# An earlier weight load and a later slot for weight sums in a gated attention and gMLP kernel

## The chip, the cores and the metric

The kernel runs on one core of a Trainium2 (trn2) chip. The metric is the device time of one execution in microseconds (us), lower is better. Engines: PE is TensorE (matmuls), DVE is VectorE, ACT is ScalarE, SP is SyncE, which here issues the DMAs. "Granted clock" is the share of full speed that TensorE was allowed in an execution.

## The reference

The result mixes a sliding-window dilated attention (32 heads, window 8, dilation 2) with a gMLP block, row by row, by a sigmoid gate. S is 2048, D is 1024, half the gMLP width is 1792.

```python
qkv = x @ wqkv                                   # attention over 8 keys, 2 apart
attn = softmax(q . k[s - 2*w] * Dh**-0.5)        # w = 0..7, masked at the start
a = (attn . v[s - 2*w]) @ wo
z = gelu(x @ w_in)                               # [2048, 3584]
z1, z2 = z[..., :1792], layernorm(z[..., 1792:])
g = w_sp @ z2 + b_sp[:, None]                    # the "spatial" product
b = (z1 * g) @ w_out
return gate * a + (1 - gate) * b
```

## The kernel before

All large products are done as Strassen-type blocks: seven products of four matmuls in place of eight. That costs additions on DVE: sums of the weights before the products (line 577), and additions of a PSUM bank and a shared term between them (line 506, in `plus`). PE may go on accumulating into that bank only when `plus` is done.

```python
def chain(...):                                   # one block of seven products
    def plus(out, a):
        dve(N / 960.0 + 0.14, clock["PE"] + 0.2)
        last_add[0] = nc.vector.tensor_tensor(out[:, n], a[:, n], vs, ALU.add)   # line 506
    # ...
    product(Y, pairs(S2, T2), False, N)
    with tc.high_priority():
        plus(Z, Y)
    # ... later a product accumulates into Z

def sums4_steps(s_out, a11, a12, a21, a22):       # sums of weights, line 577
    # four nc.vector.tensor_tensor
```

While it is built, the kernel runs a small list scheduler with a clock of its own for each engine. It decides which piece of attention work (maxima of the scores, weights, products with v: lines 671 to 717) or which sum of weights comes next on DVE. The order it finds is fixed in the program. An instruction that waits holds up all behind it: in the trace of before DVE stood 2.79 us at a sum whose weights had not landed, and did nothing else.

```python
def dve(dur, ready):
    if live[0]:
        advance(ready)            # fill DVE with other work that starts before `ready`
    return take("DVE", dur, ready)

def advance(t):
    while True:
        # ...
        events += [(max(o[0], clock["DVE"]) + FR * o[1], 2 + n, o) for n, o in enumerate(options())]
        events = [v for v in events if v[0] <= t]
        # ... the smallest goes next; `fill` holds the sums of weights
```

The sums of the z2 weights enter that list when their load has landed by the planned clock:

```python
def landed(t):
    land[0] += 1
    if land[0] == KT:
        fill.extend((t + LATE, 1.05, f) for f in wz_sums(p))
```

The z1 stage runs seven passes (fp = 0 to 6). During it SP also issues transposes of w_sp (`load_raw`), stores z1 (`z_d` in the trace) and loads further w1 blocks; ahead of the transposes it stores the result of attention (`o_d`):

```python
RAW_AT = {2: {2: 0, 4: 1, 6: 2}, 3: {4: 3, 6: 4}, 4: {2: 5, 4: 6, 6: 7}}
for fp in range(NFH):
    # ...
    run(z1_quad(fp, 0), z1_quad(fp, 1), hooks={..., **{n: lambda a=a: load_raw(0, a) for n, a in RAW_AT.get(fp, {}).items()}}, step=...)
    # ...
    if fp in (0, 2):
        load_w1(fp + 3)                           # two halves of 512 KB
```

After the eight transposes DVE forms the sums of the spatial weights: lines 1126 and 1127, later 1129 and 1130.

Of the kernel before, what the change touches and what calls it, by code (L numbers as in the profile page):

```python
# [27 lines left out]
ZC = 448  # L28
# [30 lines left out]
def kernel(  # L59
# [177 lines left out]
    def pe(dur, ready=0.0):  # L237
        return take("PE", dur, ready)
# [3 lines left out]
    def table(name):  # L242
        if tables[0] != name:
            take("ACT", 1.28)
        tables[0] = name
        return 0.0

    def act(dur, ready):
        if live[0]:
            advance(ready)  # L250
        return take("ACT", dur, ready)
# [6 lines left out]
    def dma(ready, dur, f, landed=None, timed=False):  # L258
        if not live[0]:
            return f()  # L260
        item = [ready, dur, f, landed, timed]
        due.append(item)
        return item
# [297 lines left out]
    def run(*quads, hooks={}, step=None):  # L561
        quads = list(quads)
        n = 0
        while quads:
            n += 1
            if n in hooks:
                hooks[n]()
            for q in list(quads):
                if next(q, 0) == 0:
                    quads.remove(q)  # L570
                elif step is not None:
                    step()

    def sums4_steps(s_out, a11, a12, a21, a22):
        args = ((s_out[0], a21, a22, ALU.add), (s_out[1], s_out[0], a11, ALU.subtract), (s_out[2], a11, a21, ALU.subtract),
                (s_out[3], a12, s_out[1], ALU.subtract))
        return [lambda a=a: nc.vector.tensor_tensor(*a) for a in args]  # L577
# [9 lines left out]
    def mark(bs, N=512, lo=0):  # L587
        for b in bs:
            pe((N - lo) / 2400.0)
            nc.tensor.matmul(b[:, lo:N], xT[:, 4, 0:P], xT[:, 4, 0:N - lo], start=(lo == 0), stop=True, skip_group_check=True)  # L590
# [48 lines left out]
        sync.dma_start(v_t, bass.AP(tensor=v_d.tensor, offset=v_d.offset + (g * (S + 16) + 2) * C, ap=[[NJ * C, P], [1, NJJ * C]]))  # L639


    FR, LATE = 0.4, 0.5
    t_bands, t_v = [FAR] * NG, [FAR] * NG
    sub_end, exp_end = [FAR] * NG, [FAR] * NG
    v_data = [0.0]
# [97 lines left out]
    weighed, fill = [0], []  # L743
# [42 lines left out]
    def drain():  # L786
        t = clock["PE"]
        while any(s[1] != () for s in streams) or due:
            t += 0.5
            advance(t)  # L790
# [10 lines left out]
    def load_wz(p):  # L801
        def part(k):
            for m in range(2):
                sync.dma_start(wz[p][m][:, k:k + 1], win_v[:, k:k + 1, FH + ZC * (2 * m + p):FH + ZC * (2 * m + p + 1)])
        return [lambda k=k: part(k) for k in range(KT)]


    def wz_sums(p):
        w = wz[p]
        return sums4_steps(wzs[p], w[0][:, 0:4], w[0][:, 4:8], w[1][:, 0:4], w[1][:, 4:8])  # L810
# [27 lines left out]
    def w1_half(fp, f):  # L838
        return w1_first[:, f] if fp == 0 else w1_pairs[(fp - 1) // 2 % 2][f][:, :, (fp - 1) % 2 * P:((fp - 1) % 2 + 1) * P]

    def load_w1(fp):
        for f in range(2):
            to = w1_first[:, f] if fp == 0 else w1_pairs[(fp - 1) // 2 % 2][f]
            sync.dma_start(to, win_v[:, :, HF * f + fp * P:HF * f + (fp + (2 if fp else 1)) * P])

# [17 lines left out]
    def square(n, x, junk):  # L863
        c = slice(x * HF, (x + 1) * HF)
        src = z2[:, z2_row(n), c]
        if junk is None:
            junk, src = z2[:, 7:16:8, ZC:2 * ZC], src.rearrange("p (a c) -> p a c", a=2)
        else:
            junk = junk[:, c]
        return nc.scalar.activation(junk, src, ACT.Square, accum_out=(s2, s2h)[x][:, n:n + 1])  # L870
# [109 lines left out]
    def step():  # L980
        advance(clock["PE"])
# [6 lines left out]
    def load_later(p, at, gap):  # L988
        land = [0.0]

        def landed(t):
            land[0] += 1
            if land[0] == KT:
                fill.extend((t + LATE, 1.05, f) for f in wz_sums(p))
        for n, f in enumerate(load_wz(p)):
            dma(at + gap * n, 0.65, f, landed, True)

# [46 lines left out]
    for n in range(0, len(quads), 2):  # L1044
        p, i = quads[n]
        if p == 1 or quads[n + 1][0] == 1:
            t = clock["PE"]
# [21 lines left out]
    def moments(n):  # L1069
        sl = slice(n, n + 4)  # L1070
        s1v = s1[:, 4 * n:4 * (n + 4)].rearrange("p (i c) -> p i c", c=4)
        nc.vector.tensor_tensor(s2[:, sl], s2h[:, sl], s2[:, sl], ALU.add)
        nc.vector.tensor_reduce(mean[:, sl], s1v, AX.X, ALU.add)
        nc.vector.tensor_scalar(mean[:, sl], mean[:, sl], 1.0 / FH, None, ALU.mult)
        nc.vector.tensor_tensor(var[:, sl], mean[:, sl], mean[:, sl], ALU.mult)
        nc.vector.scalar_tensor_tensor(var[:, sl], s2[:, sl], 1.0 / FH, var[:, sl], ALU.mult, ALU.subtract)
        nc.vector.tensor_scalar(var[:, sl], var[:, sl], 0.0, EPS, ALU.max, ALU.add)
        nc.gpsimd.tensor_tensor(rstd[:, sl], var[:, sl], cm05[:, sl], ALU.pow)
        fill.extend((clock["DVE"] + 2.5, 0.7, lambda m=m: normalize(m)) for m in range(n, n + 4))
# [29 lines left out]
    def load_raw(c, a):  # L1109
        row = 4 * c + (a % 4) + 8 * (a // 4)  # L1110
        inst = sync.dma_start_transpose(raw_slots[c][:, :, a, :], wsp_v[row])
        if c:
            tc.add_manual_dep(inst.ins, last_store[0].ins.name, NOSYNC, reason="behind the stores")
# [27 lines left out]
    z1s_slots = [[free(o + 2048 * r, 2048).rearrange("p (f a t) -> p f a t", f=2, a=2) for r in range(2)] for o in (T1_OFF, R_OFF + 16384)]  # L1141
    zv_slots = [free(R_OFF + 20480 + 1024 * r, 1024, F32) for r in range(2)]

    w1_left = [0]

    def w1_sums(fp):
        def one(f):
            f()
            w1_left[0] -= 1
        steps = [(0.0, 0.34, lambda f=f: one(f)) for f in w1_steps(fp)]  # L1150
        w1_left[0] += len(steps)
        fill[:0] = steps
# [5 lines left out]
    def z1_quad(fp, c):  # L1158
        a, b, s = w1_half(fp, 0), w1_half(fp, 1), ws_slots[fp % 2]
        z1s, vs = z1s_slots[fp == 3][c], zv_slots[c]  # L1160
        lo, hi = slice(512 * c, 512 * c + 512), slice(1024 + 512 * c, 1536 + 512 * c)

        def share(*a):
            last_share[0] = nc.vector.tensor_copy(*a)

        def gelu(f, a, bank):
            act(0.6 + table("gelu"), max(clock["PE"], clock["DVE"] if f + a == 2 else 0.0) + 0.2)
            last_gelu[0] = nc.scalar.activation(z1s[:, f, a, :], bank[:], ACT.Gelu_apprx_tanh)  # L1168

        def store():  # L1170
            dst = z1_d[c].rearrange("p (f t) -> p f t", f=NF)[:, fp:fp + NFH + 1:NFH, :]
            last_store[0] = sync.dma_start(dst, z1s.rearrange("p f a t -> p f (a t)"))

        return chain([a[:, k] for k in K4], [a[:, 4 + k] for k in K4], [b[:, 4 + k] for k in K4],
                     *[[s[:, q, k, :] for k in K4] for q in range(4)],
                     [xT[:, k, lo] for k in K4], [xT[:, 4 + k, lo] for k in K4], [xT[:, 4 + k, hi] for k in K4],
                     *[[x[:, k, lo] for k in K4] for x in xts], vs, gelu, nc.scalar.copy if fp < 2 else share, 512, lean=True, done=store)
# [4 lines left out]
    def z1_step(fp, at):  # L1182
        step()
        at[0] += 1
        if at[0] % 2 == 0 and squares:
            act(0.5, clock["PE"])
            square(*squares.pop(0), z1_junk)
        n = ready[0]
        if all(s[1] == () for s in streams) and n + 4 <= (squares[0][0] if squares else 16):
            fill.append((clock["ACT"] + 0.5, 1.0, lambda n=n: moments(n)))  # L1190
            ready[0] += 4
        if fp == NFH - 1 and at[0] == 2:
            fill.extend((0.0, 1.15, f) for f in wsp_sums(0, 1))

    mark([b[1] for b in bank_roles], 512, ZC)
    dma(clock["PE"] + 1.0, 2.9, lambda: load_w1(1), w1_landed(1))
    RAW_IN = 3.0
    DRAIN, SUMS = 1, NFH - 2
    RAW_AT = {2: {2: 0, 4: 1, 6: 2}, 3: {4: 3, 6: 4}, 4: {2: 5, 4: 6, 6: 7}}
    for fp in range(NFH):  # L1200
        while w1_left[0]:
            advance(max(clock["PE"], clock["DVE"]) + 0.5)
        if 0 < fp < NFH - 1:
            w1_sums(fp + 1)
        if fp == SUMS:
            fill.extend((clock["PE"] + RAW_IN, 1.15, f) for f in wsp_sums(0, 0))
        late = () if fp else [b[2] for b in bank_roles]
        at = [0]
        run(z1_quad(fp, 0), z1_quad(fp, 1), hooks={3: lambda: mark(late, 512, ZC), **{n: lambda a=a: load_raw(0, a) for n, a in RAW_AT.get(fp, {}).items()}},
            step=lambda: z1_step(fp, at))  # L1210
        if fp == DRAIN:
            drain()
        if fp in (0, 2):
            load_w1(fp + 3)
        if fp == NFH - 3:
            load_rows()
    while fill:
# [426 lines left out]
```

## Time and profile before

| | before |
|---|---|
| time of four runs | 656.74, 656.4, 658.04, 656.42 us |
| profiled span | 654.3 us |
| two stops of PE for line 506, near 193 and 325 us | 1.30 and 1.50 us |
| DVE waiting for the z2 weights and for the fifth w1 block | 2.79 and 3.78 us |

The lines behind this table stand in the prediction. This is DVE's timeline of the kernel before around the first stop (columns: start in us, time of the group in us, engine, line, operation, output and input, count; in brackets idle time before the group and what ended it):

```profile
191.81 0.29 DVE L692 TENSOR_TENSOR att_A<-att_L,att_r 128x256 f16<-128x256 f16 x1
192.02 1.22 DVE L712 TENSOR_TENSOR arena<-arena 128x2048 f16<-128x2048 f16 x1
193.16 1.16 DVE L506 TENSOR_TENSOR psum_all<-psum_all,arena 128x448 f32<-128x448 f32 x2
194.22 1.22 DVE L712 TENSOR_TENSOR arena<-arena 128x2048 f16<-128x2048 f16 x1
```

The addition that PE waits for starts at 193.16. One 1.14 us step of attention work (line 712, from 192.02 to 193.16) stands directly ahead of it, and a second one directly behind.

### The profile page before, as it was taken

What the parts mean: (1) busy time and instruction counts of PE and PEld (TensorE: products, weight loads), DVE (VectorE), ACT (ScalarE), POOL (GpSimd) and SP (SyncE); (2) the same over time, 40 slices, a digit from 0 to 9 for tenths busy, and PEclk for the clock granted to TensorE, in tenths of its full rate; (3) what the DMA queues carried; (4) which work ended last, traced back from release to release, by engine and by line L of the source; (5) the groups of instructions that cost most, each with busy time, mean ns of one, the idle gap of its engine ahead of it and who ended that gap; (6) DMA issues with size and microseconds to landing.
All of it is one profiled execution on the core that took longest, in us unless ns stands there. A gap on an engine that the chain in (4) does not pass through costs nothing.

```text
span 654.3 us, 11411 instructions
## 1 busy us (share of the span) xinstructions
PE 644.7 (99%) x4425; PEld 338.6 (52%) x4425; DVE 517.6 (79%) x820; ACT 298.3 (46%) x652; POOL 6.2 (1%) x15
## 2 busy tenths in 40 slices
PE   8999999999989999999999999999999999999998
PEld 4544467544445555444444444444444444868684
DVE  2533989999899999999799676887659999596862
ACT  4545677766677777799544212111121112202020
POOL 1000000000000000001000000000000000000000
PEclk9999999999999999999999999999999999999999
DMA  9988645697778003247995587559587465454501
GB/s 218 189 207 225 123 101 151 154 233 162 183 187 221 7 6 120 65 129 199 278 220 172 123 171 175 143 147 282 128 186 173 98 145 97 113 146 111 132 29 53
DMA packets 230198, 98.19 MB, mean 150 GB/s; under 512 B 177520, under 2 KB 217088, under 8 KB 230144
## 3 DMA queue, kind: packets, MB, share of 16 engines
q1 hardware_dynamic: 229856, 97.27, 61.7%
q8 instruction: 34, 0.56, 0.4%
q10 hardware_dynamic: 288, 0.20, 0.1%
q14 instruction: 20, 0.16, 0.1%
HBM read 45.10 MB, written 36.61 MB: 125 GB/s over the span
## 4 chain that ended last, share of the span: by engine, by line
PE 86%; DVE 5%; ACT 4%; DMA 2%; issue 1%; SPq 0%; DVEq 0%; ACTq 0%
PE psum_all L435 67%; PE psum_all L1468 8%; PE psum_all L294 7%; PE psum_all L304 3%; DMA arena<-in_B_w_in_dram 2%; ACT arena L870 1%; DVE arena L708 1%; PE psum_all L356 1%; ACT arena L1168 1%; DVE arena L577 1%; DVE psum_all L506 1%; DMA arena<-in_A_x_dram 1%; DVE arena L712 1%; ACT arena L815 0%; ACT arena L364 0%
## 5 line engine op out<-in xcount | busy, mean ns | idle before, releaser
L435 PE MATMUL psum_all<-arena 128*128 128x512 f16 (+6 forms) x2462 | 493.0, 362 | 3.9 <-DVE psum_all L506 2.8
L435 PEld LDWEIGHTS <-arena 128*128 128x128 f16 (+1 forms) x2462 | 239.7, 98 | 249.6 <-issue 5.7
L708 DVE TENSOR_TENSOR arena<-arena,att_A 128x2048 f16<-128x2048 bf16 x64 | 75.3, 1219 | 0.3
L294 PE MATMUL psum_all<-arena 128*128 128x512 bf16 x256 | 57.5, 379 | 0.0
L506 DVE TENSOR_TENSOR psum_all<-psum_all,arena 128x512 f32<-128x512 f32 (+1 forms) x74 | 48.0, 667 | 7.1 <-PE psum_all L435 4.9
L1468 PE MATMUL psum_all<-arena 128*128 128x256 f16 (+1 forms) x468 | 51.6, 273 | 0.0
L1468 PEld LDWEIGHTS <-arena 128*128 128x128 f16 x468 | 45.8, 98 | 5.5
L453 ACT COPY psum_all<-psum_all 128x512 f32<-128x512 f32 (+1 forms) x24 | 12.5, 519 | 67.2 <-PE psum_all L435 66.4
L815 ACT ACTIVATE arena<-psum_all 128x448 bf16<-128x448 f32 x64 | 34.3, 546 | 18.4 <-PE psum_all L435 9.0
L1168 ACT ACTIVATE arena<-psum_all 128x512 bf16<-128x512 f32 x56 | 31.0, 616 | 23.0 <-PE psum_all L435 8.0
L294 PEld LDWEIGHTS <-arena 128*128 128x128 bf16 x256 | 24.4, 98 | 28.4 <-issue 0.2
L712 DVE TENSOR_TENSOR arena<-arena 128x2048 f16<-128x2048 f16 x32 | 38.0, 1217 | 0.0
L364 ACT CAST arena<-psum_all 128x1988 f16<-128x1988 f32 (+3 forms) x25 | 34.0, 1359 | 2.7 <-PE psum_all L356 2.2
L577 DVE TENSOR_TENSOR arena<-arena 128x512 f16<-128x512 bf16 (+3 forms) x52 | 25.5, 521 | 7.1 <-DMA arena<-in_B_w_in_dram 6.6
L870 ACT ACTIVATE arena<-arena 128x896 bf16<-128x896 bf16 x32 | 30.9, 982 | 0.0
L297 ACT CAST arena<-psum_all 128x512 bf16<-128x512 f32 x32 | 18.8, 586 | 26.6 <-PE psum_all L294 26.5
L477 ACT COPY psum_all<-psum_all 128x512 f32<-128x512 f32 (+1 forms) x24 | 12.4, 518 | 37.5 <-PE psum_all L435 36.8
L581 DVE TENSOR_TENSOR arena<-arena 128x1024 f16<-128x1024 f16 (+2 forms) x17 | 12.1, 719 | 18.6 <-PE psum_all L435 15.7
L464 ACT COPY psum_all<-psum_all 128x512 f32<-128x512 f32 (+1 forms) x24 | 12.4, 517 | 25.8 <-PE psum_all L435 24.8
L459 ACT COPY arena<-psum_all 128x512 f32<-128x512 f32 (+1 forms) x24 | 12.7, 533 | 25.0 <-PE psum_all L435 22.9
L518 ACT COPY psum_all<-psum_all 128x512 f32<-128x512 f32 (+1 forms) x37 | 20.6, 573 | 5.0 <-PE psum_all L435 4.3
L304 PE MATMUL psum_all<-arena 128*128 128x385 bf16 x128 | 22.6, 327 | 0.0
(112 smaller groups left out, 521.5 us busy)
## 6 DMA issues: line engine op xcount, KB each, us to landing
arena<-v_d SPq DMA_DIRECT2D x8, 960.0 KB, 7.5
z_d<-arena SPq DMA_DIRECT2D x14, 512.0 KB, 4.0
arena<-z_d SPq DMA_DIRECT2D x14, 512.0 KB, 4.3
zg_d<-arena SPq DMA_DIRECT2D x56, 128.0 KB, 2.2
arena<-zg_d SPq DMA_DIRECT2D x32, 224.0 KB, 3.3
band_d<-arena SPq DMA_DIRECT2D x28, 248.5 KB, 4.1
arena<-in_A_wqkv_dram SPq DMA_DIRECT2D x16, 256.0 KB, 4.7
o_d<-arena SPq DMA_DIRECT2D x4, 1024.0 KB, 5.9
```

Of the source, the lines that this page charges most:

```text
L294: nc.tensor.matmul(ps[:], w[:, t, kt, :], xT[:, kt, 512 * c:512 * (c + 1)], start=(kt == 0), stop=(kt == KT - 1))
L304: nc.tensor.matmul(ps[:, 0:VP + 1], xT[:, kt, i * P:(i + 1) * P], wvp[:, kt, :], start=(kt == 0), stop=(kt == KT - 1))
L364: nc.scalar.copy(dst, src)
L435: nc.tensor.matmul(bank[:, 0:N], lhsT, rhs, start=(start and m == 0), stop=(m == n - 1), skip_group_check=True)
L506: last_add[0] = nc.vector.tensor_tensor(out[:, n], a[:, n], vs, ALU.add)
L577: return [lambda a=a: nc.vector.tensor_tensor(*a) for a in args]
L708: lambda ws=ws, in0=in0, in1=in1: tt(p5[:, ws], in0[:, ws], in1[:, ws], ALU.mult)), False
L712: lambda a=p3[:, ws], b=p3[:, ws.start + 4:ws.stop + 4]: tt(a, a, b, ALU.add)), not n
L815: nc.scalar.activation(z2[:, i + 8 * a, ZC * c:ZC * (c + 1)], bank[:, 0:ZC], ACT.Gelu_apprx_tanh, accum_out=s1[:, 4 * n + c:4 * n + c + 1])
L870: return nc.scalar.activation(junk, src, ACT.Square, accum_out=(s2, s2h)[x][:, n:n + 1])
L1168: last_gelu[0] = nc.scalar.activation(z1s[:, f, a, :], bank[:], ACT.Gelu_apprx_tanh)
L1468: nc.tensor.matmul(bank[:, h], l, r, start=(start and m == 0), stop=(m == len(ab) - 1), skip_group_check=True)
```

## The change

It has two parts. **Part 1** loads the fifth w1 block as its slot frees: one half inside the third pass, the other right after it, with the third transpose moved to the next pass and the two stores of this pass kept until after the loads. **Part 2** moves the ready time of the z2 sums 3.5 us later in the scheduler's clock. Neither adds or removes work.

```diff
-    FR, LATE = 0.4, 0.5
+    FR, LATE, WZ_LATE = 0.4, 0.5, 4.0
 ...
-                fill.extend((t + LATE, 1.05, f) for f in wz_sums(p))
+                fill.extend((t + WZ_LATE, 1.05, f) for f in wz_sums(p))
 ...
-        def store():
+        def store(now=False):
+            if fp == 2 and not now:
+                kept_stores.append(store)
+                return
 ...
-    RAW_AT = {2: {2: 0, 4: 1, 6: 2}, 3: {4: 3, 6: 4}, 4: {2: 5, 4: 6, 6: 7}}
+    RAW_AT = {2: {2: 0, 4: 1}, 3: {2: 2, 4: 3, 6: 4}, 4: {2: 5, 4: 6, 6: 7}}
 ...
+        if fp == 2:
+            hooks[6] = lambda: load_w1(5, (0,))
 ...
-        if fp in (0, 2):
-            load_w1(fp + 3)
+        if fp == 0:
+            load_w1(3)
+        if fp == 2:
+            load_w1(5, (1,))
+            for f in kept_stores:
+                f(True)
```

More of the change, by code (lines that the diff above doesn't have):

```diff
@@ L839, in w1_half, with load_w1 @@
         return w1_first[:, f] if fp == 0 else w1_pairs[(fp - 1) // 2 % 2][f][:, :, (fp - 1) % 2 * P:((fp - 1) % 2 + 1) * P]
-    def load_w1(fp):
-        for f in range(2):
+    def load_w1(fp, halves=(0, 1)):
+        for f in halves:
             to = w1_first[:, f] if fp == 0 else w1_pairs[(fp - 1) // 2 % 2][f]
@@ L1142 @@
     zv_slots = [free(R_OFF + 20480 + 1024 * r, 1024, F32) for r in range(2)]
-    w1_left = [0]
+    w1_left, kept_stores = [0], []
     def w1_sums(fp):
@@ L1208 @@
         at = [0]
-        run(z1_quad(fp, 0), z1_quad(fp, 1), hooks={3: lambda: mark(late, 512, ZC), **{n: lambda a=a: load_raw(0, a) for n, a in RAW_AT.get(fp, {}).items()}},
-            step=lambda: z1_step(fp, at))
+        hooks = {3: lambda: mark(late, 512, ZC), **{n: lambda a=a: load_raw(0, a) for n, a in RAW_AT.get(fp, {}).items()}}
+        if fp == 2:
+            hooks[6] = lambda: load_w1(5, (0,))
+        run(z1_quad(fp, 0), z1_quad(fp, 1), hooks=hooks, step=lambda: z1_step(fp, at))
         if fp == DRAIN:
             drain()
-        if fp in (0, 2):
-            load_w1(fp + 3)
+        if fp == 0:
[4 more added lines that the diff above has]
+                f(True)
         if fp == NFH - 3:
```

## The prediction

> **What bounds the kernel now.** I read the page first, then TensorE's waits, then the timelines around the two largest, then the chain that ended last.
>
> ```profile
> PE 644.7 (99%) x4425; PEld 338.6 (52%) x4425; DVE 517.6 (79%) x820; ACT 298.3 (46%) x652; POOL 6.2 (1%) x15
> PEclk9999999999999999999999999999999999999999
> ```
>
> TensorE (PE) is busy for 99% of a 654.3 us span at full granted clock. A change that removes no matmul can only remove what is left of PE's idle time. The waits of PE between 186 and 330 us:
>
> ```profile
> PE psum_all L435 <- DVE psum_all L506: 2.8, 2, 1.5
> PE psum_all L435 <- ACT psum_all L518: 0.3, 1, 0.3
> ```
>
> Two stops, 2.8 us together, both for the VectorE (DVE) addition of line 506, which must read a PSUM bank before PE may accumulate into it. After 325 us the timeline of PE shows no further stop up to 651 us. So the change can win 2.8 us at most, 0.43%. PE's timeline places the stops:
>
> ```profile
> 193.84 69.77 PE L435 MATMUL psum_all<-arena 128*128 128x448 f16 x368 [1.30 <-DVE psum_all L506]
> 325.32 4.91 PE L435 MATMUL psum_all<-arena 128*128 128x512 f16 x22 [1.50 <-DVE psum_all L506]
> ```
>
> DVE is late in both because, in its fixed order, it had stood at sums (line 577) of weights still in flight:
>
> ```profile
> 167.40 1.22 DVE L708 TENSOR_TENSOR arena<-arena,att_A 128x2048 f16<-128x2048 bf16 x1
> 171.42 2.22 DVE L577 TENSOR_TENSOR arena<-arena 128x1792 f16<-128x1792 bf16 x2 [2.79 <-DMA arena<-in_B_w_in_dram]
> 173.55 0.28 DVE L671 TENSOR_TENSOR att_m<-att_L 128x256 f16<-128x256 f16 x1
> ...
> 320.60 1.55 DVE L577 TENSOR_TENSOR arena<-arena 128x512 f16<-128x512 bf16 x4 [3.78 <-DMA arena<-in_B_w_in_dram]
> ```
>
> First the z2 weights (2.79 us), then the fifth w1 block (3.78 us). The change addresses these two waits.
>
> **What the Trainium skill says.** "Perfetto Trace Analysis", section "DMA Instruction — HWDGE (DVE, Sync)": a DMA's record on the issuing engine covers descriptor generation, not the movement of data, which may begin before the record ends when descriptors overfill the buffer. The trace agrees: the weight transpose issued at 332.8 us has a record of 2.14 us and lands after 5.0. The same page, "What "DMA-bound" means": an issuing sequencer whose track is solid DMA slices is one of the forms. SyncE (SP) is such a track here:
>
> ```profile
> 303.17 8.19 SPq L195 DMA_TRANSPOSE arena<-in_B_w_sp_dram  x3
> 311.46 1.20 SPq L190 DMA_DIRECT2D z_d<-arena  x2
> 312.76 2.39 SPq L190 DMA_DIRECT2D arena<-in_B_w_in_dram  x2
> 315.20 7.54 SPq L195 DMA_TRANSPOSE arena<-in_B_w_sp_dram  x2
> ```
>
> "DMA: Bandwidth & Descriptors", section "Rules for kernel authors", advises issuing a DMA early and waiting on its semaphore late; the change does half of this in each place. "VectorE: DVE Perf Modes", section "The perf-mode tier table", has 1224 ns for a 2048-element 16-bit tensor_tensor; the trace has 1219 ns for line 708.
>
> **Part 1, the w1 block.** Nothing is added or removed: the same two 512 KB loads, four stores and eight transposes before the same point. Before, SP issues three transposes, two stores, then the loads at 312.8 and 313.8; the last lands 6.8 us later, at 320.6. After, only two transposes stand ahead. Three took 8.19 us, the third starting at 308.5, so the loads start at about 308.5 and 309.6. Their slots are free: one pass of z1 is 14 products of 4 matmuls at 0.216 us, 12.1 us, and the third pass ends near 304.7. With the same 5 to 6.8 us they land between 314.5 and 316.5. DVE reaches the sums when its four normalizations end, 314.12 + 2.71 = 316.83. So its wait of 3.78 goes, and with it PE's stop of 1.50. Up to 2.3 us of lateness would still be harmless (3.78 - 1.50).
>
> Does the win last? Here the next wait takes its place. The sums of the spatial weights (line 1126) need all eight transposes:
>
> ```profile
> 337.97 1.23 DVE L1126 TENSOR_TENSOR arena<-arena 128x2048 f16<-128x2048 bf16 x1 [0.69 <-issue]
> ...
> 351.07 1.22 DVE L1130 TENSOR_TENSOR arena<-arena 128x2048 f16<-128x2048 bf16 x1
> 352.21 1.29 DVE L506 TENSOR_TENSOR psum_all<-psum_all,arena 128x512 f32<-128x512 f32 x2
> ```
>
> The last transpose lands at 332.8 + 5.0 = 337.8; line 1126 starts at 337.97 after 0.69 us of idling that the view calls issue. Its semaphore record on DVE lasts 1.72 us and ends there, so I take the idling as waiting for the transpose. From there to 353.5 DVE runs without a gap. When does PE need the addition at 352.21? From 325.32 its next products lie 4 x 0.216 = 0.863 us apart; the seventh product of the last pass (first half) is number 32 from there: 325.32 + 32 x 0.863 = 352.94. The first addition ends at about 352.21 + 0.69 = 352.90. **The margin is already zero.** If the transposes land no sooner, PE can run up to 1.5 us ahead after 325 and must give it all back by 353: an estimated 0.35 us near 341 and the rest near 353. And they should land no sooner: from 303.2 SP has no gap to 336.5, the windows of 3 us from 306 to 342 show a DMA share of 1.02 to 1.24, and the same bytes stand ahead of the last transpose in both kernels. The first transpose waits for the o_d store, which waits for the end of attention on DVE (297.56). So part 1 alone is worth about 0 us, and part 2 counts as far as it moves the end of attention.
>
> **Part 2, the z2 sums.** Only a ready time in the scheduler's own estimated clock changes, by 3.5 us: four instructions of about 1.05 us go later in DVE's order. What takes the place of the wait at 168.6? From the code: the scheduler picks the lowest of ready time plus 0.4 of the duration. Call its clock after the product at 167.40 zero. Before, it picked two sums (planned 1.05 each), then the maxima (line 671), then two sums. So the maxima were ready for it later than 1.05 + 0.42 - 0.08 = 1.39, and no later than 2.10 + 0.42 - 0.08 = 2.44. That the sums had lost to the previous product (1.135) puts their ready time after -1.10, now after 2.40. So after: second product (to 1.135); then a third (to 2.27) if the maxima are ready after 1.51, which is most of that interval; then the maxima; then sums. On the chip two products end at 168.55 + 2 x 1.14 = 170.83. But the maxima read scores whose second load is issued at 170.3 and lands 2.5 us later, at 172.8. **A wait of 2.0 us takes the place of the 2.79 us one:** DVE gains about 0.75. With one product ahead it would idle 3.2 us and lose 0.4.
>
> The addition at 193.16 follows attention work without a gap, so it comes 0.75 sooner and PE's stop falls from 1.30 to 0.55. PE has no other gap to 263, the 0.28 us stop there hangs on work that shifts along, and DVE waits 1.36 us for PE before 285.56; so the end of attention, the transposes and the margin at 353 all shift by the same 0.75.
>
> **Sum.** 0.75 from part 2 and about 0.05 from part 1, since the margin at 352.94 is only known to a tenth: 0.8 us, against the 2.8 that the list of waits promises. 656.74 - 0.8 = 655.9.
>
> **Rivals.** (a) Both stops vanish and the time stays won: 653.9. For it: the list of waits, and that PE sees no stop after 325. Against: the zero margin at 353, which costs no time now and so is in no list. (b) Part 2 wins its whole 1.30 us, the maxima falling behind three products or the scores landing earlier, and part 1 nothing: 655.4. The order cannot be seen in the trace, so this keeps real weight. (c) Reordering the queue moves the last transpose itself by a microsecond either way, since its predecessors took 2.1 to 5.1 us to issue under the same pressure: 655 to 657. Nothing in the trace says which way. (d) The delay holds also for the second z2 weights (sums at 210.33 to 215.8); they could finish behind the quads that need them. The kernel drains them before those quads, and DVE has attention work of the same length to swap in, so I expect nothing; a miss would cost under 1 us.
>
> **Range and chances.** The middle is 655.9. (a) sets the low end, which I cut to 654.4 because the zero margin must then be wrong; a lost 0.4 in part 2 with (c) against it gives 657.3. The three timings of before lie 1.6 us apart, which alone asks for such width. Two per cent is 13 us, far over any of these: faster 0.01, same 0.98, slower 0.01.
>
> **What would show it.** Part 1 right: line 577 near 317 without idling behind the w1 load; the stop near 325 gone. The give-back right: line 1126 waiting longer than 0.69, still 0.2 us after the last transpose, and new PE stops for line 506 near 341 and 353. Part 2 right: two line 708 products, then line 671 after an idle stretch that ends with the score load at about 172.8; a PE stop near 193 of about half a microsecond. Wrong: if the transposes land over 1 us sooner against the end of attention, the time falls to 654.5 or less; if line 671 stands behind three products, to 655.4.

## The result, and the profile after

| | before | after |
|---|---|---|
| median of four runs | 656.58 us | 654.37 us |
| the four runs | 656.74, 656.4, 658.04, 656.42 | 654.45, 654.28, 655.0, 654.11 |
| profiled span | 654.3 us | 652.7 us |

The ratio is 0.9963 with a 95% interval of 0.9946 to 0.998. Here and below a ratio is the mean time of one kernel's fast runs over the mean of the other's in the same rounds, so it is not quite the ratio of the medians. The change is worth 2.2 us by the medians where 0.8 us was predicted (a median of 655.9). By the 2% measure the class is "same".

Read PE's waits of the kernel after first, in the same stretch, 186 to 360 us:

```profile
PE psum_all L435 <- DVE psum_all L506: 0.8, 1, 0.8
```

One stop of 0.8 us is left of two with 2.8 us together. PE's timeline says which one. It is neither of the old two:

```profile
187.36 75.18 PE L435 MATMUL psum_all<-arena 128*128 128x448 bf16 x396
...
270.50 79.98 PE L435 MATMUL psum_all<-arena 128*128 128x512 f16 x362
351.30 20.88 PE L435 MATMUL psum_all<-arena 128*128 128x512 f16 x94 [0.81 <-DVE psum_all L506]
```

Both stops of before, at 193 and 325 us, have vanished in this trace (the first one comes back in later traces of the same kernel, see below): two blocks of matmuls run through those places without a gap. A new stop stands at 351. The busy time on the page must not be compared with the one of before:

```profile
PE 640.9 (98%) x4379; PEld 338.4 (52%) x4425; DVE 517.4 (79%) x820; ACT 297.9 (46%) x652; POOL 6.2 (1%) x15
```

PE shows 4379 matmuls against 4425 weight loads: 46 records of matmuls are missing from this trace, so the 3.8 us less busy time is no gain. Counts are to be checked before busy times are compared.

DVE's timeline of the kernel after at the two waits, and around 193:

```profile
168.03 2.36 DVE L708 TENSOR_TENSOR arena<-arena,att_A 128x2048 f16<-128x2048 bf16 x2
172.28 0.29 DVE L671 TENSOR_TENSOR att_m<-att_L 128x256 f16<-128x256 f16 x1 [1.90 <-DMA att_L<-band_d]
...
174.58 4.21 DVE L577 TENSOR_TENSOR arena<-arena 128x1792 f16<-128x1792 bf16 x4
...
191.55 0.29 DVE L692 TENSOR_TENSOR att_A<-att_L,att_r 128x256 f16<-128x256 f16 x1
191.76 1.16 DVE L506 TENSOR_TENSOR psum_all<-psum_all,arena 128x448 f32<-128x448 f32 x2
192.82 2.35 DVE L712 TENSOR_TENSOR arena<-arena 128x2048 f16<-128x2048 f16 x2
...
315.64 1.54 DVE L577 TENSOR_TENSOR arena<-arena 128x512 f16<-128x512 bf16 x4
```

The sums of the z2 weights at 174.58 no longer wait, and the maxima at 172.28 wait 1.90 us for the scores instead: a wait for a wait, as foreseen. But look at 191.76: the addition now stands ahead of both steps of line 712. Part 2 changed the order 20 us behind the place it was aimed at. Last, at 315.64 the w1 sums start with no idle time before them.

The queue of SP shows why, and the lines of the spatial sums show the price:

```profile
302.30 4.85 SPq L195 DMA_TRANSPOSE arena<-in_B_w_sp_dram  x2
307.25 1.21 SPq L190 DMA_DIRECT2D arena<-in_B_w_in_dram  x2
308.55 2.76 SPq L190 DMA_DIRECT2D z_d<-arena  x2
311.37 10.54 SPq L195 DMA_TRANSPOSE arena<-in_B_w_sp_dram  x3
```

```profile
336.36 1.22 DVE L1126 TENSOR_TENSOR arena<-arena 128x2048 f16<-128x2048 bf16 x1 [1.83 <-issue]
...
349.42 1.22 DVE L1130 TENSOR_TENSOR arena<-arena 128x2048 f16<-128x2048 bf16 x1
350.55 1.29 DVE L506 TENSOR_TENSOR psum_all<-psum_all,arena 128x512 f32<-128x512 f32 x2
```

The w1 loads are issued at 307.25, behind two transposes instead of three. The last of the eight transposes lands at 336.18, line 1126 idles 1.83 us for it (0.69 before), DVE then has no gap up to the addition at 350.55, and PE stops 0.81 us for that addition. That is the give-back that the prediction described.

The stops thus account for the spans: 1.30 and 1.50 gone, 0.81 new, 1.99 us in sum, where the spans differ by 1.6 and the medians by 2.2.

### The profile page after: what moved, and what is told of

Same layout as the page of the kernel before. It is cut to its first block, busy times and chain, and to the rows that moved or that the text cites. A ratio compares the mean times of both kernels' runs of the same rounds, so it can differ in the third digit from the quotient of the medians.

```text
span 652.7 us, 11363 instructions
## 1 busy us (share of the span) xinstructions
PE 640.9 (98%) x4379; PEld 338.4 (52%) x4425; DVE 517.4 (79%) x820; ACT 297.9 (46%) x652; POOL 6.2 (1%) x15
## 4 chain that ended last, share of the span: by engine, by line
PE 91%; ACT 5%; DVE 2%; issue 1%; DMA 1%; SPq 0%; ACTq 0%; DVEq 0%
PE psum_all L435 69%; PE psum_all L294 8%; PE psum_all L1477 8%; PE psum_all L304 3%; ACT arena L870 1%; PE psum_all L356 1%; ACT arena L1168 1%; PE psum_all L822 1%; DMA arena<-in_A_x_dram 1%; ACT arena L364 1%; DVE psum_all L506 1%; ACT arena L815 1%; ACT psum_all L518 0%; PE psum_all L590 0%; SPq L162 0%
## 5 line engine op out<-in xcount | busy, mean ns | idle before, releaser
L294 PE MATMUL psum_all<-arena 128*128 128x512 bf16 x245 | 55.8, 379 | 1.1 <-issue 0.8
L1168 ACT ACTIVATE arena<-psum_all 128x512 bf16<-128x512 f32 x56 | 31.2, 615 | 21.9 <-PE psum_all L435 15.0
```

The costliest lines, as they stand in the source:

```text
L294: nc.tensor.matmul(ps[:], w[:, t, kt, :], xT[:, kt, 512 * c:512 * (c + 1)], start=(kt == 0), stop=(kt == KT - 1))
L1168: last_gelu[0] = nc.scalar.activation(z1s[:, f, a, :], bank[:], ACT.Gelu_apprx_tanh)
```

## The experiments

Eighteen runs of eleven kernels were made on five chips (named by number), each job beside runs of the kernel before on the same chip. All gave correct results. In the table, "mean" is the mean of the runs whose granted clock is recorded as 1.000, minus the same for the kernel before in the same job.

| run | chip | edit | median us (before) | ratio [95%] | mean, us |
|---|---|---|---|---|---|
| part1_alone | 11 | part 1 only | 655.24 (657.24) | 0.9979 [0.996, 0.9998] | -1.7 |
| part1_again | 5 | the same | 655.45 (655.99) | 0.9995 [0.9972, 1.0018] | -0.6 |
| part2_alone | 11 | part 2 only | 655.91 (657.24) | 0.9984 [0.9966, 1.0001] | -1.4 |
| part2_again | 5 | the same | 654.05 (655.99) | 0.9971 [0.9953, 0.9989] | -1.7 |
| after_again | 5 | whole change | 653.63 (655.99) | 0.9973 [0.9952, 0.9993] | -1.8 |
| after_third | 9 | whole change | 654.53 (656.97) | 0.9962 [0.9935, 0.9989] | -1.7 |
| after_fourth | 15 | whole change | 654.75 (657.55) | 0.9955 [0.9933, 0.9976] | -2.2 |
| one_product_behind | 11 | before, 712 behind 506 | 656.03 (657.24) | 0.9983 [0.9965, 1.0001] | -1.1 |
| behind_second | 9 | the same | 656.06 (656.97) | 0.9979 [0.9954, 1.0004] | -0.5 |
| product_put_back | 11 | after, 712 ahead again | 655.28 (657.24) | 0.9974 [0.9959, 0.9988] | -1.7 |
| put_back_second | 9 | the same | 656.11 (656.97) | 0.9988 [0.9961, 1.0015] | -0.2 |
| sums_behind | 4 | after, two spatial sums later | 653.2 (655.2) | 0.9972 [0.996, 0.9984] | -1.8 |
| sums_behind_second | 9 | the same | 654.27 (656.97) | 0.9955 [0.9931, 0.9979] | -2.1 |
| part1_sums_behind | 4 | part 1 and that | 655.07 (655.2) | 0.9991 [0.9978, 1.0004] | -0.6 |
| before_sums_behind | 4 | before and that | 655.05 (655.2) | 1.0011 [0.999, 1.0032] | +0.2 |
| transposes_later | 4 | after, one more load ahead | 655.14 (655.2) | 0.9999 [0.9987, 1.0012] | -0.1 |
| sum_between | 15 | best order | 653.54 (657.55) | 0.9942 [0.9921, 0.9964] | -3.1 |

The eighteenth, before_look, was one untimed look at the kernel before. Differences of 1 us are hardly resolved by such times, so most verdicts below rest on the traces: an order is exact there, and the intervals used below repeat to about 0.02 us. One rule ties them to the time. In the 16 usable traces (all but that of one_product_behind, see below) with a granted clock of 0.999 or more, the span minus all of PE's stops over 0.25 us (after the first 20 us) is 649.5 to 650.5 us. So a kernel here is as fast as its stops are short. Three usable traces with a granted clock of 0.997 (part1_alone, part1_again, before_sums_behind) need 651.8 to 652.1 us for the same and are left out where spans are compared.

**Theory after the result.** (A) The gain at 193 has two halves: less idling, and one line 712 moved behind the addition. (B) Part 1 keeps most of its stop at 325, since the transposes usually land soon enough. **Rivals.** (A') the waits alone made the gain at 193 (scores landed sooner). (B') the zero margin at 353 eats part 1, and the gain is part 2's.

### The parts, each alone

```diff
 # part1_alone, part1_again: the kernel after, but
-    FR, LATE, WZ_LATE = 0.4, 0.5, 4.0
+    FR, LATE, WZ_LATE = 0.4, 0.5, 0.5
 # part2_alone, part2_again: the kernel before, but
-    FR, LATE = 0.4, 0.5
+    FR, LATE, WZ_LATE = 0.4, 0.5, 4.0
-                fill.extend((t + LATE, 1.05, f) for f in wz_sums(p))
+                fill.extend((t + WZ_LATE, 1.05, f) for f in wz_sums(p))
```

> Part 1 alone: the early w1 halves, with the z2 sums where they were. Gate theory (the eighth transpose of the spatial weights decides when PE passes the last z1 product): the stop near 325 us (1.50) goes, the stop near 193 (1.30) stays, and most of the 1.5 us is given back in a new stop near 352, so the time is 0.3 to 0.7 us under before, and the last transpose lands only that much sooner. Rival (the two stops are independent and additive): 1.5 us under before, no stop near 352.

> Part 2 alone: the later slot for the z2 sums, with the w1 loads where they were. Gate theory: the stop near 193 is gone, the stop near 325 stays at 1.5, the end of attention and all transposes come 1.3 to 1.4 us sooner, and the time is 1.3 to 1.4 us under before. Rival of the prediction on record: only 0.75 us under before, with about 0.55 us of the stop near 193 left.

> Part 1 alone, on one chip with part 2 alone and the whole change. Additive theory: 1.4 to 1.7 us under before, no stop near 325, a stop near 351 only if the transposes took over 34 us. Gate theory: under 0.5 us.

> Part 2 alone. Both theories: 0.7 to 1.4 us under before; the stop near 193 between 0 and 0.9, larger where the score load lands later (wait of line 671: 1.9 us in the first trace of the changed kernel, 3.4 in the first of this one).

> The whole change. Additive theory: the sum of the two parts measured beside it to within 0.5 us, so 2.2 to 3 us under before. Gate theory: less than the sum by about 1 us, and a stop near 351.

By the means both parts have a gain of their own: part 1 1.7 and 0.6 us (the second not resolved from nothing), part 2 1.4 and 1.7 us. On chip 5, where both parts and the whole ran together, the parts add up to 2.3 and the whole is 1.8, the same within such noise. So rival B' falls in its strict form; part 1 is not worth zero. PE and then DVE in part2_again:

```profile
187.17 75.07 PE L435 MATMUL psum_all<-arena 128*128 128x448 bf16 x396
...
322.71 49.59 PE L435 MATMUL psum_all<-arena 128*128 128x512 f16 x229 [0.27 <-DVE psum_all L506]
```

```profile
317.99 1.56 DVE L577 TENSOR_TENSOR arena<-arena 128x512 f16<-128x512 bf16 x4 [2.54 <-DMA arena<-in_B_w_in_dram]
```

Here part 2 alone removes the stop near 193 and leaves the one at the w1 sums. It does not always do the first: in part2_alone, where the scores landed at 173.12 us and not at 171.57 as here, 0.81 us of the stop stayed. The second is only 0.27 here, after a wait of 2.54, where it was 1.50 after 3.78 in the first trace. The stop is the wait less about 2.3 us, in five traces with the old order of the loads: 3.78 and 1.50, 3.42 and 1.14, 3.40 and 1.12, 3.17 and 0.88, 2.54 and 0.27. So what part 1 can win is set by how late the load lands in that execution.

### The kernel before, looked at again

No edit.

> The kernel before once more, for a second profile of it on the chip of the next three. Every trace so far agrees with: span = about 650.2 us + the TensorE stops over 0.25 us after 20 us (+1.7 where the granted clock was 0.997). Fixed-gate theory (prediction on record): the eight transposes take 34.6 us from the landing of the o_d store to the last landing, as in the first trace, to within 0.3. Rival, formed from the first eight runs: that length is not fixed but varies by 2 us from run to run (32.1 to 34.6), so the margin near 353 was zero only in the first trace; here it is 0 to 2.5 us. The stops near 193 and 325 are 0.8 to 2.7 and 0.9 to 1.5 in either case.

```profile
193.95 69.77 PE L435 MATMUL psum_all<-arena 128*128 128x448 f16 x368 [1.39 <-DVE psum_all L506]
...
271.69 100.62 PE L435 MATMUL psum_all<-arena 128*128 128x512 f16 x463
```

```profile
319.30 1.56 DVE L577 TENSOR_TENSOR arena<-arena 128x512 f16<-128x512 bf16 x4 [2.38 <-DMA arena<-in_B_w_in_dram]
```

The same program on another chip: its first stop is there again (1.39), its second is not (PE runs from 271.69 for 100 us without one), since the w1 wait was 2.38. And its last transpose landed 36.6 us after the issue of the o_d store, where it was 40.2 us in the first trace of before. The prediction had taken that second number as fixed. The expectations above missed too: no stop near 325 where 0.9 to 1.5 was expected, and from landing to landing 31.2 us, which is outside both theories.

### One step of line 712 moved by itself

```diff
 # one_product_behind, behind_second: the kernel before, but for the first pair of z2 blocks
-            dve(N / 960.0 + 0.14, clock["PE"] + 0.2)
+            dve(N / 960.0 + 0.14, clock["PE"] + 0.2 - (early.pop(0) if early else 0.0))   # early = [0.6, 0.6]
 # product_put_back, put_back_second: the kernel after, but there
-            dve(N / 960.0 + 0.14, clock["PE"] + 0.2)
+            early and early.pop() and pull(streams[2]); dve(N / 960.0 + 0.14, clock["PE"] + 0.2)   # pull: issue the next product step first
```

The first changes the order of DVE's instructions in this alone:

```
 L692 TensorTensor att_A<-att_L_107,att_r 128x8x8x4
-L712 TensorTensor arena<-arena 128x2048
-L506 TensorTensor psum_all<-psum_all,arena 128x448 x2
-L712 TensorTensor arena<-arena 128x2048
+L506 TensorTensor psum_all<-psum_all,arena 128x448 x2
+L712 TensorTensor arena<-arena 128x2048 x2
```

and the second changes the kernel after in the opposite way alone (the step goes ahead of line 692 too).

> The kernel before with one single edit: the line 712 addition that stands ahead of the first z2 addition (line 506) goes behind it; sums and loads stay where they were, so DVE still waits 2.79 us for the z2 weights. Order theory (the stop near 193 went because one 1.14 us attention step changed places with the addition): the stop falls from 1.30 to about 0.1 to 0.2 and the time by 1.1 to 1.2 us. Rival (the stop went because DVE stood idle less): the stop stays near 1.30 and the time is that of before.

> The changed kernel with that one line 712 step put back ahead of the first z2 addition; sums late, loads early as changed. Order theory: a stop of 0.6 to 0.8 us comes back near 193, everything after it shifts, and the time is 0.6 to 0.8 us over the changed kernel (about 655.1). Rival (less idling alone removed the stop): no stop near 193 and the time of the changed kernel.

> The kernel before with only that step moved behind the addition. Order theory: the stop near 193 is 1.2 us smaller than that of before in the same DMA conditions, so 0.1 to 0.3, and the time 0.9 to 1.2 us under before. Idling theory: stop of 1.3 and time of before.

> The changed kernel with the one line 712 step back ahead of the first z2 addition. Order theory: the addition comes 1.2 us later against PE than in the changed kernel, so a stop of 0.6 to 1.3 near 193 where the changed kernel has none to 0.1, and 0.6 to 1.2 us over the changed kernel in time. Idling theory (the stop went because DVE waits 1.9 us instead of 2.8): no stop, and the time of the changed kernel within 0.3 us.

DVE and then PE of behind_second (the order of before, with the step behind):

```profile
173.28 2.22 DVE L577 TENSOR_TENSOR arena<-arena 128x1792 f16<-128x1792 bf16 x2 [4.05 <-DMA arena<-in_B_w_in_dram]
...
193.90 1.16 DVE L506 TENSOR_TENSOR psum_all<-psum_all,arena 128x448 f32<-128x448 f32 x2
194.96 2.35 DVE L712 TENSOR_TENSOR arena<-arena 128x2048 f16<-128x2048 f16 x2
```

```profile
194.57 70.10 PE L435 MATMUL psum_all<-arena 128*128 128x448 f16 x368 [1.58 <-DVE psum_all L506]
```

From the first sum to the addition is 193.90 - 173.28 = 20.62 us. In the four traces with the order of before whose maxima, as here, do not wait, it is 21.73 to 21.75 (193.16 - 171.42 = 21.74 in the first). The step is worth **1.12 us**. That PE still stops 1.58 us here, where 0.1 to 0.3 was expected, has another reason (unmoved, the step would have made it 1.58 + 1.12 = 2.70 us by this): the weights came late in this execution (4.05 us of waiting), and so did other loads in traces of this chip.

DVE and PE of put_back_second (the kernel after, with the step ahead again):

```profile
175.13 0.29 DVE L671 TENSOR_TENSOR att_m<-att_L 128x256 f16<-128x256 f16 x1 [4.58 <-DMA att_L<-band_d]
...
194.28 1.22 DVE L712 TENSOR_TENSOR arena<-arena 128x2048 f16<-128x2048 f16 x1
195.41 0.28 DVE L692 TENSOR_TENSOR att_A<-att_L,att_r 128x256 f16<-128x256 f16 x1
195.62 1.15 DVE L506 TENSOR_TENSOR psum_all<-psum_all,arena 128x448 f32<-128x448 f32 x2
```

```profile
196.29 3.94 PE L435 MATMUL psum_all<-arena 128*128 128x448 f16 x20 [3.10 <-DVE psum_all L506]
```

In the order of after, the addition starts a fixed time after the scores land (the second score load, for which line 671 waits): 19.57 us in all nine traces with that order, within 0.01, for landings between 171.57 and 173.72. With the step put back it is 20.58 and 20.59: **1.02 us** more. The stops, 2.04 and 3.10 us, are larger than expected (0.6 to 0.8 and 0.6 to 1.3), since the scores landed at 173.75 and 175.03. In time, putting it back cost 1.45 us against after_third in the same job (means at full clock 656.21 and 654.76). On chip 11 no run of the whole change stood beside it, and its -1.7 alone decides nothing. Theory A holds against A': less idling is not all. The swap is a bit over 1 us of it. Whether the idling adds a second half is taken up in step 5 below.

One run is unusable as a trace. The profiled execution of one_product_behind took 2116.95 us; its other five runs took 654.74 to 656.98. Its page and a group of PE's timeline:

```profile
PE 2110.9 (100%) x4425; PEld 682.2 (32%) x4425; DVE 532.3 (25%) x820; ACT 313.9 (15%) x652; POOL 6.2 (0%) x15
```

```profile
599.23 21.69 PE L294 MATMUL psum_all<-arena 128*128 128x512 bf16 x26
```

Matmuls of 512 columns stood 21.69 / 26 = 0.83 us apart here, in place of 0.216; from 1363 us on they stood 0.62 us apart. That run is left out of its ratio and mean.

### Is the margin at 353 what limits part 1?

```diff
 # sums_behind (+_second), part1_sums_behind, before_sums_behind: after, part 1 alone, before; each with
-        if fp == NFH - 1 and at[0] == 2:
+        if fp == NFH - 1 and at[0] == 4:
             fill.extend((0.0, 1.15, f) for f in wsp_sums(0, 1))
 # transposes_later: the kernel after; the b_sp row is loaded ahead of the last three transposes
+        if fp == 4:
+            hooks[1] = lambda: sync.dma_start(bsp_bc, ...)    # and no longer in load_rows
```

The first moves one line 1129 and one line 1130 behind the last additions of z1, so that late transposes have some 2.3 us more room (two steps of 1.14). The second makes the transposes late on purpose.

> The changed kernel with two of the eight sums of the spatial weights (one line 1129, one line 1130) moved behind the last two line 506 additions of the last z1 pass. Gate theory: the additions then come about 2.3 us sooner, the stop of 0.81 near 351 goes, and the time is 0.7 to 0.8 us under the changed kernel (about 653.6). Rival (the stop near 351 is slack that a later stage would absorb, or another wait takes its place): within 0.3 us of the changed kernel.

> Part 1 alone, with the same two sums moved behind the additions. Gate theory: what part 1 wins near 325 is no longer given back, so 1.4 to 1.6 us under before, about 1 us under part 1 alone. Rival: as part 1 alone.

> The kernel before with the same two sums moved behind the additions and nothing else. Gate theory: the margin at 353 was zero but no wait, so nothing is won: within 0.2 us of before. Rival (the order of these sums costs time by itself): up to 0.8 us under before.

> The changed kernel with one 512 KB load (the b_sp row, needed only in the next stage) moved from behind the transposes to ahead of the last three. Gate theory: the last transpose lands 1 to 2 us later, the stop near 351 grows by as much, and the time grows by the same amount (655.5 to 656.5). Rival (the transposes are hidden): time of the changed kernel within 0.3 us.

> The changed kernel with two sums of the spatial weights behind the last additions of z1. If the additions near 351 limit PE only in runs where the transposes land late: 0 to 0.4 us under the changed kernel on average and no stop near 351 in any trace. If they limit PE in every run: 0.7 us or more under it.

Room alone did little: part 1 with it is 0.6 us below before (not resolved from nothing), before with it 0.2 above, and the whole change with it 0.4 below after_third on chip 9, also not resolved. The margin is zero, but it seldom binds. Lateness does bind, as DVE and PE of transposes_later show:

```profile
336.72 1.23 DVE L1126 TENSOR_TENSOR arena<-arena 128x2048 f16<-128x2048 bf16 x1 [2.17 <-issue]
```

```profile
338.61 12.25 PE L435 MATMUL psum_all<-arena 128*128 128x512 f16 x55 [0.32 <-DVE psum_all L506]
351.67 20.66 PE L435 MATMUL psum_all<-arena 128*128 128x512 f16 x93 [0.81 <-DVE psum_all L506]
```

With line 1126 idling 2.17 us PE stops twice, 1.13 us together, and the whole gain is gone (-0.1 us where sums_behind in the same job has -1.8; that one has the two sums moved as well, and the kernel after itself did not run on this chip). These are the two places and about the sizes that the prediction named. Twelve traces have the new order of the loads and nothing delayed. In the eight of them that keep the order of the sums, line 1126 idled from nothing to 1.83 us, and only the 1.83 made a stop of 0.25 us or more; the next, 0.87 in product_put_back, made none. So B holds as a rule, and the first trace of after was the exception.

Why does a margin of zero seldom bind? DVE of before_look shows it:

```profile
342.57 1.23 DVE L1129 TENSOR_TENSOR arena<-arena 128x2048 f16<-128x2048 bf16 x1 [0.32 <-PE psum_all L435]
...
350.91 1.29 DVE L506 TENSOR_TENSOR psum_all<-psum_all,arena 128x512 f32<-128x512 f32 x2
```

In all 14 traces that keep the order of the sums, the addition starts 8.33 to 8.34 us after this line 1129, and PE's next use of the bank 0.74 to 0.75 us after that, whether PE stops there or not. So the margin is zero in before_look too, although its last transpose landed at 334.3 us and not at 337.8. But here line 1129 waits 0.32 us for PE: DVE has time in hand ahead of it, and a late transpose uses that up first. The zero margin belongs to the order; the room for the transposes is the time that DVE waits for PE ahead of it.

### The whole change on further chips, and a better order

```diff
 # sum_between: the kernel after with `at[0] == 4` and `early` from above, and
-    FR, LATE, WZ_LATE = 0.4, 0.5, 4.0
+    FR, LATE, WZ_LATE = 0.4, 0.5, 1.5
```

> The whole change once more, as the yardstick of the next three on one chip. Both theories: 1.8 to 2.5 us under before, no stop near 193 or 325; a stop near 351 only if the last transpose lands over 39 us after the o_d store is issued (39.7 in its first trace: 0.81; 38.4 in its second: none).

> Sums_behind with the z2 sums at a slot between (late by 1.5 in place of 4.0): two products, one sum, the maxima, three sums, two products; the first z2 addition still stands ahead of both line 712 steps. Score theory (in the changed kernel's order the first z2 addition starts 19.57 us after the score load lands, in all eight traces that have it): with one sum of 1.05 us moved ahead of the maxima it starts 18.4 to 18.6 us after that landing, and the stop near 193 is 1.05 us smaller in late-landing runs, none in others; 0 to 1 us under the changed kernel on average. Rival (the new slot brings back the wait for the weights, or later reorderings cost as much): same time as the changed kernel or over it.

> The changed kernel beside it on the same chip: 1.5 to 2.5 us under before; first z2 addition 19.57 us after the score landing, within 0.1; a stop near 193 equal to that addition's lateness.

With 1.5 one sum goes ahead of the maxima, where DVE would idle, and three behind. DVE of after_fourth and then DVE and PE of sum_between, both on chip 15:

```profile
173.82 0.29 DVE L671 TENSOR_TENSOR att_m<-att_L 128x256 f16<-128x256 f16 x1 [3.61 <-DMA att_L<-band_d]
...
193.29 1.16 DVE L506 TENSOR_TENSOR psum_all<-psum_all,arena 128x448 f32<-128x448 f32 x2
```

```profile
172.19 1.09 DVE L577 TENSOR_TENSOR arena<-arena 128x1792 f16<-128x1792 bf16 x1 [1.88 <-DMA arena<-in_B_w_in_dram]
173.19 0.28 DVE L671 TENSOR_TENSOR att_m<-att_L 128x256 f16<-128x256 f16 x1
...
191.53 1.16 DVE L506 TENSOR_TENSOR psum_all<-psum_all,arena 128x448 f32<-128x448 f32 x2
```

```profile
187.27 75.07 PE L435 MATMUL psum_all<-arena 128*128 128x448 bf16 x396
```

The addition starts 18.49 us after the scores land (173.04 in this trace), 1.08 less than in the kernel after, and PE does not stop. The kernel after still stops 1.34 us here, since its scores landed at 173.72, 0.68 us later than in sum_between. sum_between is 0.8 us faster than after_fourth at full clock (653.95 and 654.78) and beats both kernels; it contains the moved spatial sums too, whose share is not separated.

The expectation of no stop near 193 failed in after_third, whose scores landed at 173.59 us (PE):

```profile
193.84 70.10 PE L435 MATMUL psum_all<-arena 128*128 128x448 f16 x368 [1.41 <-DVE psum_all L506]
```

So of the four traces of the kernel after two have no stop near 193 (scores at 172.19 and 172.43 us) and two have 1.41 and 1.34 us.

The whole change was run on three further chips: its medians lie 2.4 to 2.8 us under those of before, its means at full clock 1.7 to 2.2 us. Part of the difference is the runs of before at clock 0.997, four of eleven on chip 15.

## Why the prediction was wrong

Taken by its own steps:

1. **The cause and the ceiling: right.** Two late additions, made late by two waits. Both stops vanished in the first trace of after; in four of the nine traces with its order around 193 a first stop of 0.81 to 1.41 us stayed.
2. **Part 1 up to 325: right.** Two transposes ahead, loads from 307.25 (predicted 308.5), sums at 315.64 without idling. The slack it worked out, 2.3 us, is the offset between wait and stop in five traces.
3. **"So part 1 alone is worth about 0 us": the second step that failed.** The term was 0.05 us; in the first pair of traces it measured 1.50 - 0.81 = 0.69. It rested on "And they should land no sooner", the last transpose as late against the o_d store as in the one trace at hand, 40.2 us after its issue. The first traces of before and after, with 40.2 and 39.7 us, proved to be the late ones: apart from transposes_later, delayed on purpose to 40.0, the 16 other usable traces have 36.6 to 38.9 us. The mechanism is right: the new stop near 353 came (351.30, 0.81 us) and the deliberate delay brought both predicted stops. Only in the after trace did it take back 0.81 of 1.50. In typical executions part 1 keeps its whole stop at 325. That stop itself is not always 1.50: in six traces with the old order of the loads it is 1.50, 1.14, 1.12, 0.88, 0.27 and under 0.25, 0.8 on average. Times of part 1 alone are 0.6 and 1.7 us.
4. **The waits at 170: right in the size, by luck.** A score wait of 1.90 (predicted 2.0) took the place of the weight wait. But one product went ahead of the maxima and not two, the branch for which the prediction had "it would idle 3.2 us and lose 0.4". DVE began the pair of products 0.63 us later and the scores landed 0.60 us sooner (172.19, not 172.79) in this trace, and 3.2 - 0.63 - 0.60 = 1.97.
5. **"The addition at 193.16 follows attention work without a gap, so it comes 0.75 sooner": the first step that failed.** It took the order up to the addition as unchanged. Against PE's last group of two matmuls before this block (line 590, at 186.70 before and 186.98 after) the addition came 1.68 us sooner: 6.46 before, 4.78 after. Of this 1.02 to 1.12 is the step of line 712 that went behind, and about 0.6 the shorter idling, predicted as 0.75. The stop is that distance less 5.16 us: 1.30 before, none after, with 0.38 to spare. With the step put back it would be 4.78 + 1.02 - 5.16 = 0.64, close to the predicted 0.55. The unseen swap is the term that was missing. The idling term was met by luck. With the step behind in both orders, the addition would come 20.80 us after the last z2 load lands in the order of before (20.62 + 0.18), and it comes 19.57 us after the scores land in that of after. With the two landings of the first trace of before (171.24 and 172.79 us) the exchange of one wait for the other then loses 0.3 us: 192.04 against 192.36. With the pairs of landings of 16 traces it is worth between -0.4 and +0.5 us, 0.1 on average, and in the three with the latest scores it loses about 1.0. This is an estimate from the intervals, and it takes the landings as independent of the order. By it, what part 2 wins over many executions is the swap.
6. **The sum.** Predicted 0.75 + 0.05 = 0.8. In the first pair of traces 1.30 + 1.50 - 0.81 = 1.99. On chips 5 and 4 the first stop falls from 1.39 and 1.54 to none, but elsewhere some of it stays. Over the traces with a granted clock of 0.999 or more it averages 1.41 in three with the order of before and 0.51 in nine with that of after, 0.9 less; the second averages 0.8. That is 1.7 us together, on mixed chips, near the 1.6 of the first spans and the means at full clock (1.7 to 2.2).
7. **The rivals.** The result is nearest to (a), both stops won; its 653.9 lies 0.5 below the median, and the trace of after has 0.81 us given back. (b) was right that part 2 would win its 1.30, for a reason it did not name. For (c), the last transpose came 38.5 us after the o_d store on average in twelve traces with the new order and 38.0 in six with the old; nothing to be told apart. For (d), no trace shows a stop for the second z2 weights; no run isolates them.

What stays open: why the same program's loads land up to 4.6 us apart between chips and executions (the second score load at 171.6 to 176.2 us, of which 2.9 us is a later issue), and how much part 1 alone is worth to better than 1 us.

## What to carry to other kernels

When a scheduler fixes the order, one changed ready time can reorder instructions 20 us further on. Before a gain is sized, look at what stands directly ahead of the late instruction on its engine: a step of 1.1 us there was worth more than the idling that the change saved there (about 0.6 in the first pair of traces, about nothing over all). And a margin of zero costs nothing as long as the engine waits for the other ahead of it: measure that wait, and look at the kernel before twice, best on two chips, before a limit built from one landing time is subtracted in full.

## What the Trainium skill lacked or had wrong

- No page gives the spread of a load's landing from one execution to the next. "DMA: Bandwidth & Descriptors", section "Latency and other measured facts", gives 0.2 us on average and 2 us at high load for the access to HBM. Here the second score load of the same stage landed between 171.6 and 176.2 us of the span, 4.6 us apart, where its issue began at 169.22 and 172.07, so that from issue to landing it took 2.4 and 4.2 us; and the last transpose landed 36.6 to 40.2 us after the o_d store.
- None of the pages read has the small clock state met here, a granted clock of 0.997 in some executions of several of these kernels. Three traces with it take 651.8 to 652.1 us besides PE's stops, against 649.5 to 650.5 us; 0.3% of 650 us is 2.0 us.
- "TensorE: Matmul & The Clock Gate", section "Seeing it yourself", warns that clock records can be unreliable and that the clock has been seen at a quarter for 50 us and more. One execution here ran its matmuls of 512 columns 0.84 us apart up to 1363 us and 0.62 us apart from there to its end at 2115.2 us, in place of 0.216, with a recorded granted clock of 1.000.
